# A planned order of instructions: other rates for transfers within device memory, and a slack for GpSimd

## The chip, the cores and the metric

The kernel runs on one core of one Trainium2 chip. The metric is the time of one execution in microseconds (us), as the device measures it. Three runs of the kernel before gave a median of 778.36 us (777.24 to 778.53).

The engines have short names in the profile: PE is TensorE's matmuls, PEld its weight loads, DVE is VectorE, ACT is ScalarE, POOL is GpSimd and SP is SyncE. POOLq and SPq are the queues on which POOL and SP issue transfers.

## The reference

All arrays are fp32; S = 2048, D = 512, F = 1792.

```python
x = A_x                                             # [1, 2048, 512]
g = sigmoid((x * gate_w).sum(-1, keepdims=True))
a = einsum("bsd,ed->bse", x, dft_hid_re)            # Fourier transform along D
b = einsum("bsd,ed->bse", x, dft_hid_im)
y = einsum("ts,bse->bte", dft_seq_re, a) - einsum("ts,bse->bte", dft_seq_im, b)   # along S, the real part
gate, up = x @ W_gate, x @ W_up
h = where(gate > 0, gate, 0) * up
return g * y + (1 - g) * (h @ W_down)
```

## The kernel before, in words

**Products.** Every fp32 operand is split into a high and a low part in a rounded form (ACT copies the high part, DVE subtracts for the low part), and a product is three passes of TensorE: high-high, high-low, low-high. A product of two by two blocks is made from seven block products (numbered 1 to 7) in place of eight, so sums and differences of blocks are formed on the way, of the weights, of x, and of the large matrices `cr` and `ci` (the transform along S). A matmul is 128 x 128 by 128 x 512.

**Stages, in TensorE's order.** First the blocks (`Block`) of gate and up: seven groups of weights times two halves q of x, with PSUM tiles named c. Each block makes two tiles h (`h0`, `h1`) and sums of them (`hs`), and `h_out` stores these to `hd` in device memory, from POOL (hd<-h, hd<-hs). Then the transform along D (tiles a, weights v, stored to `ad`), the last block, the product with W_down (`Down`, tiles z, operands hr loaded from `hd`), and then the transform along S: `Joint` 1, two `Sequence`s, `Joint` 3, two `Sequence`s, `Joint` 2 (tiles jA to jG, z).

**The sums of the large matrices.** The transform along S needs sums of blocks of `cr` and `ci`. For some of them the sums are formed long before, during the first stages, and kept in device memory as `tb`. There are two ways. `right_sums` (list `SUMS`) loads four blocks to tiles p, has DVE add them, and POOL stores them (tb<-p). `copied_sums` (list `DSUMS`, five entries) does it without the chip's own memory: POOL issues a transfer that copies a block of ci or cr to tb, and behind it a transfer that adds another block to it (`accum_op`). Four results 0, 2, 1, 3 make one entry, each a copy and an add. Result 1 begins as a copy of result 0 and result 3 as a copy of result 1 (tb<-tb), so result 0's copy and add, result 1's and result 3's follow each other, each waiting for the landing of the one before. The tb are first needed in the transform along S, at 485 us and later.

**Units.** On-chip memory is cut into 51 units of 4 KB per partition. Every tile takes a unit, and the unit of a finished tile is given to a new one. So a new tile's first write waits for the last use of the old one, which may be a store.

**Order.** The program is not run in the order in which it is written. Each step has a key: a place in time, in units of one 128 x 512 matmul of TensorE, to which it belongs. `Step` prices each step, `Queues` simulates the DMA queues (one of SP, one of POOL, which take turns packet by packet on 16 engines; a transfer lands `LANDING` us, and sometimes `BUSY` us more, after its last packet), `Plan.due` works out when each step has to be done, and `Plan.order` simulates the whole kernel and picks, for each engine, the step that can start first: when the steps it comes after are done, when its key has come (for DVE, ACT and SP 40 keys earlier, for POOL not before), and when a unit is free. Of steps that can start at nearly the same time the one that is due first goes first. What comes out is a fixed order of instructions on each engine and a fixed choice of units. On the chip each engine runs its list in order, and waits at an instruction until its inputs are there and its tile is free; what the planner supposed of times has no effect any more. In particular, a transfer on POOL that waits for another one's landing holds up the stores behind it.

`AT`, `SUMS` and `DSUMS` hold the keys that were set by hand: offsets for the opening, the weights of the opening (`w0`), the second half of x (`x`), the gate (`gate`), the transform's weights (`v`), the operands of the transform along S (`l0`, `l1`, `J1` to `J3`), the operands of a woven-in small product (`xt`), and the start of each entry of sums.

Of the kernel before, what the change touches and what calls it, by code (L numbers as in the profile page):

```python
# [11 lines left out]
OP = mybir.AluOpType  # L12
PSUM = bass.MemoryType.PSUM
DRAM = bass.MemoryType.DRAM
P = 128
# [47 lines left out]
class Buf:  # L63
# [17 lines left out]
    @property  # L81
    def all(self):
        return self[:]


class Step:


    def __init__(self, key, engine, name, a, k):
        self.key, self.engine, self.name, self.a, self.k = key, engine, name, a, k  # L90
        refs = [x for x in a if isinstance(x, Ref)]
        refs += [k[x] for x in ("out", "in_") if isinstance(k.get(x), Ref)]
        writes = [k["out"] if "out" in k else a[0]]
        if "accum_out" in k:
            writes.append(k["accum_out"])
        self.writes = [x for x in writes if isinstance(x, Ref)]
        self.reads = [x for x in refs if x is not writes[0]]
        if "accum_op" in k or name == "matmul" and not k["start"]:
            self.reads += self.writes
        self.after, self.start, self.end, self.due, self.rest = set(), None, None, None, None  # L100
        n = writes[0].size() if self.writes else 0
        self.hold = None
        if name == "tensor_copy":
            self.work = 0.1 + n * 0.52e-3
            self.hold = self.work - 0.05
        elif name == "dma_start":
            n = max(x.size() // (P if x.base.kind == "dram" else 1) for x in (*self.writes, *self.reads))
            self.work = n * 4 * P / 4096 * 0.160 / 16 * (2 if "accum_op" in k else 1)
        elif engine == "tensor":
            self.work = self.hold = 0.22667 * n / N  # L110
        elif engine == "vector":

            self.work = 0.156 + n * 1.039e-3
            self.hold = self.work - 0.083
        else:
            self.work = 0.19 + n * 0.845e-3
            self.hold = self.work - 0.09
# [8 lines left out]
class Queues:  # L126
# [32 lines left out]
    def add(self, step, start):  # L159

        def end(s, t, busy):
            s.end = t + self.LANDING + (self.BUSY if busy and t > self.EARLY else 0)

        self.now = self.serve(self.queues, self.now, max(start, self.now), end)
        packets = max(1.0, step.work / (0.160 / 16 * (2 if "accum_op" in step.k else 1)))
        self.queues.setdefault(step.engine, []).append([start, packets, step.work / packets, step])
        self.serve({e: [list(x) for x in q] for e, q in self.queues.items()}, self.now, 1e9, end)


class Plan:  # L170
# [9 lines left out]

    SUMS, STORES = 24, 0

    FREE = 30

    AHEAD = {"vector": 40, "scalar": 40, "sync": 40, "gpsimd": 0}

# [4 lines left out]
    def op(self, key, f, *a):  # L191
        self.ops.append((key, len(self.ops), f, a, self.rest))
# [58 lines left out]
    def order(self):  # L251
        todo = {}
        for s in self.steps:
            todo.setdefault(s.engine, []).append(s)
        for e in ("vector", "scalar"):
            todo[e].sort(key=lambda s: s.due)
        free, queues = dict.fromkeys(todo, 0.0), Queues()
        late, live, ends, over = 0.0, 0, [], []
        left = {b: len({id(x) for x in b.uses}) for b in self.bufs if b.kind == "unit"}
        done, begun, now = [], set(), 0.0  # L260

        turn = {s: n for n, s in enumerate(self.steps)}
        ahead = sorted(min(turn[s] for s in b.uses) for b in left if b.uses)
        while any(todo.values()):
            best = None
            for e, queue in todo.items():
                found = None
                near = queue[:1] if e == "tensor" or not queue else [*queue[:48], min(queue, key=turn.get)]
                for s in near:
                    if any(x.start is None for x in s.after):  # L270
                        continue
                    t = max(free[e], now)
                    for x in s.after:
                        t = max(t, x.end + (0 if x.engine == e else self.WAIT + 0.16 * (x.engine == "tensor")))
                    if e != "tensor":
                        t = max(t, (s.key - self.AHEAD[e] - self.FREE * (s.key > self.now - 200)) * self.MATMUL + late)
                    new = {r.base for r in (*s.writes, *s.reads) if r.base.kind == "unit" and r.base not in begun}
                    if new:
                        short = live + bisect_left(ahead, turn[s]) + len(new) - UNITS
                        if short > 0:  # L280
                            if len(ends) < short:
                                continue
                            t = max(t, ends[short - 1])
                    if found is None or t < found[0] - 0.12:
                        found = t, s, new
                if found and (best is None or found[0] < best[0]):
                    best = found
            if best is None:
                raise ValueError(f"no way on at {len(done)}: {[(e, q[0].key, q[0].name) for e, q in todo.items() if q]}")
            t, s, new = best  # L290
            now = t
            while over and ends[0] <= t:
                over.remove(min(over, key=Plan.last))
                ends.pop(0)
                live -= 1
            live += len(new)
            for b in new:
                ahead.remove(min(turn[x] for x in b.uses))
            begun |= new
            todo[s.engine].remove(s)  # L300
            s.start = t
            if s.name == "dma_start":
                free[s.engine] = t + self.ISSUE[s.engine]
                queues.add(s, free[s.engine] + self.LATE.get(s.engine, 0))
            else:
                s.end, free[s.engine] = t + s.work, t + s.hold
            if s.engine == "tensor" and s.key >= 0:
                late = max(late, t - s.key * self.MATMUL - 6 * self.MATMUL)
            for b in {r.base for r in (*s.writes, *s.reads) if r.base.kind == "unit"}:
                left[b] -= 1  # L310
                if not left[b]:
                    over.append(b)
            ends = sorted(map(Plan.last, over))
            done.append(s)
        self.steps = sorted(done, key=lambda s: s.start)
# [26 lines left out]
def kernel(ctx: ExitStack, tc, xP, xG, wgu, wd, cr, ci, wri, gw, out):  # L342
# [23 lines left out]
    dram = ctx.enter_context(tc.tile_pool(name="dram", bufs=1, space=DRAM))  # L366
# [4 lines left out]
    op, pe = plan.op, plan.pe  # L371
# [38 lines left out]
    def E():  # L410
        return plan
# [98 lines left out]
                op(key + k + 8 - (0 if n else early), w.lo, n, f)  # L510


    AT = {'open': (-19, 11, 33, 19, 97), 'w0': (17, 83, 126), 'x': (-184, -126, -85, -78, -51, -34, 35, 26), 'gate': (58, 44, 474), 'v': (-90, -80, -68, -38, -22, 4, 6, 34, 40), 'lw': (-246, -150, -138, -114, -112, -104), 'll': (-90, 62, 36, 96, 138, 176), 'l0': (-154, -58, -68, 16), 'l1': (-60, -118, -24, 40), 'z': (38,), 'J1': (88, 14, 76, 56, 116), 'J2': (174, 18, 40, 44, 52), 'J3': (168, 22, 52, 62, 52), 'hr': (52, 48, 61), 'rest': (26, 46), 'gated': (1880, 1930, 1968, 2008), 'xt': (-20, 10, 30), 'p': (62, 44, 32, 16), 'hs': (8, 6)}

    SUMS = {(0, 3, 1): 1764, (0, 1, 0): 865, (0, 2, 1): 675, (0, 3, 0): 985, (1, 1, 0): 1600, (1, 2, 1): 1602, (1, 5, 3): 1310, (1, 4, 2): 1070, (0, 4, 0): 489, (0, 1, 1): 125, (1, 4, 3): 1740}

    DSUMS = {(0, 2, 0): 290, (1, 2, 0): 100, (1, 3, 1): 427, (1, 3, 0): 645, (1, 1, 1): 520}

# [500 lines left out]
    def copied_sums(m, of, jj, key):  # L1021
        t = [tb[m, of - 1, jj, n] for n in range(4)]
        i = {b: (Joint if of < 4 else Sequence).source(m, of if of < 4 else of - 4, jj, b) for b in BLOCKS}
        for n, (o, a, b) in enumerate(((0, i["12"], i["22"]), (2, i["11"], i["12"]), (1, t[0], i["11"]), (3, t[1], i["21"]))):
            k = key + (0, 10, 50, 100)[n]
            op(k, lambda o=o, a=a: E().gpsimd.dma_start(out=t[o], in_=a, max_dma_last_dim=1024))
            op(k + 25, lambda o=o, b=b: E().gpsimd.dma_start(out=t[o], in_=b, accum_op=OP.add, max_dma_last_dim=1024))

    def gated(m, jj, g, key):
        r = buf("p")  # L1030
# [324 lines left out]
    w0, w1, w2 = Weights(0), Weights(1), Weights(2)  # L1355
# [184 lines left out]
```

## Time and profile before

| | |
|---|---|
| median of three runs | 778.36 us (777.24 to 778.53) |
| the profiled execution's own time | 779.43 us |
| its span, first to last instruction | 777.3 us |
| TensorE busy (PE) | 768.5 us (99%) |
| VectorE busy (DVE) | 697.7 us (90%) |
| ScalarE busy (ACT) | 499.7 us (64%) |
| GpSimd busy (POOL) | 140.4 us (18%) |
| DMA | 263.08 MB, 338 GB/s on the mean |
| transfers of POOL's queue (q0) | 100.15 MB, 42.3% of 16 engines' span |
| transfers of SP's queue (q1) | 162.17 MB, 54.2% |
| granted TensorE clock | 0.999 |

A row of a timeline has the start in us, the time in us, the engine, a line of the code (all steps run through one helper, so it is always the same), the operation, "out<-in" by the program's names without numbers, how many, and in brackets the idle time of the engine before it and what ended it. A row of waits has the engine and tile that waited, what for, and then us in total, how often, and the longest. A row of the DMA issues has out<-in, the queue, how many, KB each, and the median time from issue to landing. POOL and SP rows named DMA_DIRECT2D are the issuing of a transfer, not the transfer itself.

### The profile page before, as it was taken

The page shows a single profiled execution, that of the slowest core. Times are in us where ns is not written, and L with a number is a line of the kernel's source. Part 1 is how long each engine was busy: PE and PEld are TensorE (multiplying, and loading weights), DVE is VectorE, ACT ScalarE, POOL GpSimd, SP SyncE. Part 2 cuts the span into 40 slices and gives each one's busy share as a digit, 9 for nine tenths or more (in the row PEclk, how much of TensorE's full clock was granted, in tenths as well). Part 3 has the DMA queues.
Part 4 walks back from the last instruction along what each step waited for, and adds up shares of the span by engine and source line. Part 5 has one row for each costly group of instructions (what it writes and reads, how often), then busy time and mean ns, then how long its engine had stood idle before and what let it go on. Part 6 is the DMA issues. An engine that isn't in the chain of part 4 may idle for free.

```text
span 777.3 us, 10104 instructions
## 1 busy us (share of the span) xinstructions
PE 768.5 (99%) x3392; PEld 633.5 (81%) x3392; DVE 697.7 (90%) x812; ACT 499.7 (64%) x713; POOL 140.4 (18%) x204
## 2 busy tenths in 40 slices
PE   8999999999999999999999999999999999999998
PEld 6888888878788888888888888888888888888887
DVE  6999968676778986999979899999999999999997
ACT  6765574747475644666565568957567896566863
POOL 0123434342322222320202010001010001111000
PEclk9999999999999999999999999999999999999999
DMA  8966999999999899999999999999949899999993
GB/s 326 283 208 184 289 345 312 321 343 325 311 331 419 280 358 418 418 406 394 382 416 399 409 406 414 389 413 412 298 136 339 340 409 358 303 332 294 363 367 87
DMA packets 83683, 263.08 MB, mean 338 GB/s; under 512 B 8624, under 2 KB 19632, under 8 KB 83632
## 3 DMA queue, kind: packets, MB, share of 16 engines
q1 hardware_dynamic: 48048, 162.17, 54.2%
q0 software_dynamic: 35440, 100.15, 42.3%
q8 instruction: 26, 0.43, 0.2%
q14 instruction: 25, 0.20, 0.1%
q10 hardware_dynamic: 144, 0.13, 0.0%
HBM read 189.01 MB, written 94.38 MB: 365 GB/s over the span
## 4 chain that ended last, share of the span: by engine, by line
PE 74%; DMA 15%; DVE 7%; issue 2%; POOL 1%; SPq 1%; ACT 0%; POOLq 0%; DVEq 0%; ACTq 0%
PE z L123 40%; PE a L123 10%; PE c L123 10%; DMA tb<-ci 6%; PE jB L123 4%; PE jA L123 4%; DMA tb<-tb 4%; DMA tb<-cr 3%; PE jX L123 2%; PE jD L123 2%; DMA hd<-h 2%; DVE h L123 1%; PE jG L123 1%; DVE xl L123 1%; DMA wr<-wgu 1%
## 5 line engine op out<-in xcount | busy, mean ns | idle before, releaser
L123 PE MATMUL z<-cl,lh 128*128 128x512 f32 x452 | 175.9, 389 | 0.0
L123 PE MATMUL z<-ch,lh 128*128 128x512 f32 x452 | 175.8, 389 | 0.0
L123 PE MATMUL z<-ch,ll 128*128 128x512 f32 x452 | 175.8, 389 | 0.0
L123 DVE TENSOR_TENSOR jcl<-jr,jch 128x1024 fp32r<-128x1024 f32 x84 | 98.9, 1220 | 1.2 <-ACT jch L123 0.7
L123 PEld LDWEIGHTS z<-cl,lh 128*128 128x128 f32 x452 | 84.8, 188 | 17.8 <-DVE cl L123 0.2
L123 PEld LDWEIGHTS z<-ch,lh 128*128 128x128 f32 x452 | 84.8, 188 | 17.6
L123 PEld LDWEIGHTS z<-ch,ll 128*128 128x128 f32 x452 | 84.8, 188 | 17.6
L123 ACT CAST ch<-r 128x1024 fp32r<-128x1024 f32 x64 | 66.0, 1051 | 45.3 <-DVE r L123 30.5
L123 ACT CAST jch<-jr 128x1024 fp32r<-128x1024 f32 x84 | 84.3, 1052 | 8.1 <-PE z L123 3.2
L123 DVE TENSOR_TENSOR cl<-r,ch 128x1024 fp32r<-128x1024 f32 x64 | 77.2, 1220 | 0.4
L123 ACT CAST ch<-hr 128x1024 fp32r<-128x1024 f32 (+1 forms) x56 | 51.5, 944 | 31.8 <-PE z L123 17.5
L123 ACT ACTIVATE c<-c 128x512 f32<-128x512 f32 x74 | 42.8, 584 | 38.9 <-PE c L123 24.3
L123 DVE TENSOR_TENSOR cl<-hr,ch 128x1024 fp32r<-128x1024 f32 (+1 forms) x56 | 59.4, 1086 | 6.7 <-DMA hr<-hd 3.2
L123 DVE TENSOR_TENSOR p<-p,p 128x1024 f32<-128x1024 f32 x44 | 53.1, 1219 | 10.5 <-DMA p<-ci 5.5
L123 POOL DMA_DIRECT2D tb<-p x48 | 26.4, 559 | 110.1 <-DVE p L123 82.7
L123 PE MATMUL c<-xh,w1l 128*128 128x512 f32 x112 | 43.7, 390 | 1.9 <-ACT c L123 1.9
L123 PE MATMUL c<-xh,w2l 128*128 128x512 f32 x112 | 43.8, 391 | 1.6 <-DVE h L123 1.6
L123 PE MATMUL c<-xl,w1h 128*128 128x512 f32 x112 | 43.6, 389 | 0.0
L123 PE MATMUL c<-xl,w2h 128*128 128x512 f32 x112 | 43.6, 389 | 0.0
L123 PE MATMUL c<-xh,w2h 128*128 128x512 f32 x112 | 43.6, 389 | 0.0
L123 PE MATMUL a<-vh,xl 128*128 128x512 f32 x112 | 43.6, 389 | 0.0
L123 PE MATMUL a<-vl,xh 128*128 128x512 f32 x112 | 43.6, 389 | 0.0
(196 smaller groups left out, 1681.2 us busy)
## 6 DMA issues: line engine op xcount, KB each, us to landing
tb<-p POOLq DMA_DIRECT2D x48, 512.0 KB, 9.6
jr<-tb SPq DMA_DIRECT2D x48, 512.0 KB, 8.9
hr<-hd SPq DMA_DIRECT2D x36, 512.0 KB, 7.8
ad<-a POOLq DMA_DIRECT2D x28, 512.0 KB, 8.1
p<-cr SPq DMA_DIRECT2D x24, 512.0 KB, 9.6
tb<-ci POOLq DMA_DIRECT2D x24, 512.0 KB, 11.5
hd<-hs POOLq DMA_DIRECT2D x21, 512.0 KB, 10.1
r<-cr SPq DMA_DIRECT2D x21, 512.0 KB, 12.5
```

The costliest lines, as they stand in the source:

```text
L123: getattr(getattr(nc, self.engine), self.name)(*map(ap, self.a), **{k: ap(x) for k, x in self.k.items()})
```

## The change

The planner's arithmetic and its hand-set keys change; no step is added or removed. A transfer whose operands are all in device memory is priced 1.2 times as slow as one that is not (2.2 times where it adds, instead of 2). For a step on POOL that comes after a DMA, the planner counts the DMA as landed 3 us later than it otherwise would (`SLACK`; for DMAs that land after 20 us); POOL's list is ordered by that. In `copied_sums` the four copies start at keys 0, 20, 60 and 120 instead of 0, 10, 50 and 100, and an add is set 35 keys behind its copy instead of 25. Some entries of `AT`, `SUMS` and `DSUMS` move. In the list `AT`, cut here to the entries that differ:

```diff
         elif name == "dma_start":
             n = max(x.size() // (P if x.base.kind == "dram" else 1) for x in (*self.writes, *self.reads))
-            self.work = n * 4 * P / 4096 * 0.160 / 16 * (2 if "accum_op" in k else 1)
+            within = all(x.base.kind == "dram" for x in (*self.writes, *self.reads))
+            self.rate = 0.160 / 16 * ((2.2 if within else 2) if "accum_op" in k else 1.2 if within else 1)
+            self.work = n * 4 * P / 4096 * self.rate
...
-        packets = max(1.0, step.work / (0.160 / 16 * (2 if "accum_op" in step.k else 1)))
+        packets = max(1.0, step.work / step.rate)
...
+    SLACK = {"vector": 0, "scalar": 0, "gpsimd": 3}
...
                     for x in s.after:
                         t = max(t, x.end + (0 if x.engine == e else self.WAIT + 0.16 * (x.engine == "tensor")))
+                        if x.name == "dma_start" and x.end > 20:
+                            t = max(t, x.end + self.SLACK.get(e, 0))
...
-    AT = {... 'w0': (17, 83, 126), 'x': (-184, -126, -85, -78, -51, -34, 35, 26), 'gate': (58, 44, 474), 'v': (-90, -80, -68, -38, -22, 4, 6, 34, 40), 'l0': (-154, -58, -68, 16), 'l1': (-60, -118, -24, 40), 'J1': (88, 14, 76, 56, 116), 'J3': (168, 22, 52, 62, 52), 'gated': (1880, 1930, 1968, 2008), 'xt': (-20, 10, 30) ...}
-    SUMS = {... (0, 2, 1): 675, (0, 3, 0): 985, (1, 2, 1): 1602, (1, 4, 3): 1740}
-    DSUMS = {(0, 2, 0): 290, (1, 2, 0): 100, (1, 3, 1): 427, (1, 3, 0): 645, (1, 1, 1): 520}
+    AT = {... 'w0': (17, 83, 110), 'x': (-192, -134, -93, -86, -59, -42, 27, 18), 'gate': (66, 44, 474), 'v': (-90, -80, -68, -38, -22, 4, 10, 42, 44), 'l0': (-154, -42, -52, 32), 'l1': (-60, -118, -28, 40), 'J1': (88, 14, 76, 56, 124), 'J3': (168, 22, 62, 62, 52), 'gated': (1880, 1930, 1968, 2012), 'xt': (-20, 26, 62) ...}
+    SUMS = {... (0, 2, 1): 665, (0, 3, 0): 965, (1, 2, 1): 1632, (1, 4, 3): 1730}
+    DSUMS = {(0, 2, 0): 290, (1, 2, 0): 100, (1, 3, 1): 417, (1, 3, 0): 675, (1, 1, 1): 520}
...
         for n, (o, a, b) in enumerate(((0, i["12"], i["22"]), (2, i["11"], i["12"]), (1, t[0], i["11"]), (3, t[1], i["21"]))):
-            k = key + (0, 10, 50, 100)[n]
+            k = key + (0, 20, 60, 120)[n]
             op(k, lambda o=o, a=a: E().gpsimd.dma_start(out=t[o], in_=a, max_dma_last_dim=1024))
-            op(k + 25, lambda o=o, b=b: E().gpsimd.dma_start(out=t[o], in_=b, accum_op=OP.add, max_dma_last_dim=1024))
+            op(k+35, lambda o=o, b=b: E().gpsimd.dma_start(out=t[o], in_=b, accum_op=OP.add, max_dma_last_dim=1024))
```

More of the change, by code (lines that the diff above doesn't have):

```diff
@@ L510, in w_prep @@
                 op(key + k + 8 - (0 if n else early), w.lo, n, f)
-    AT = {'open': (-19, 11, 33, 19, 97), 'w0': (17, 83, 126), 'x': (-184, -126, -85, -78, -51, -34, 35, 26), 'gate': (58, 44, 474), 'v': (-90, -80, -68, -38, -22, 4, 6, 34, 40), 'lw': (-246, -150, -138, -114, -112, -104), 'll': (-90, 62, 36, 96, 138, 176), 'l0': (-154, -58, -68, 16), 'l1': (-60, -118, -24, 40), 'z': (38,), 'J1': (88, 14, 76, 56, 116), 'J2': (174, 18, 40, 44, 52), 'J3': (168, 22, 52, 62, 52), 'hr': (52, 48, 61), 'rest': (26, 46), 'gated': (1880, 1930, 1968, 2008), 'xt': (-20, 10, 30), 'p': (62, 44, 32, 16), 'hs': (8, 6)}
-    SUMS = {(0, 3, 1): 1764, (0, 1, 0): 865, (0, 2, 1): 675, (0, 3, 0): 985, (1, 1, 0): 1600, (1, 2, 1): 1602, (1, 5, 3): 1310, (1, 4, 2): 1070, (0, 4, 0): 489, (0, 1, 1): 125, (1, 4, 3): 1740}
-    DSUMS = {(0, 2, 0): 290, (1, 2, 0): 100, (1, 3, 1): 427, (1, 3, 0): 645, (1, 1, 1): 520}
+    AT = {'open': (-19, 11, 33, 19, 97), 'w0': (17, 83, 110), 'x': (-192, -134, -93, -86, -59, -42, 27, 18), 'gate': (66, 44, 474), 'v': (-90, -80, -68, -38, -22, 4, 10, 42, 44), 'lw': (-246, -150, -138, -114, -112, -104), 'll': (-90, 62, 36, 96, 138, 176), 'l0': (-154, -42, -52, 32), 'l1': (-60, -118, -28, 40), 'z': (38,), 'J1': (88, 14, 76, 56, 124), 'J2': (174, 18, 40, 44, 52), 'J3': (168, 22, 62, 62, 52), 'hr': (52, 48, 61), 'rest': (26, 46), 'gated': (1880, 1930, 1968, 2012), 'xt': (-20, 26, 62), 'p': (62, 44, 32, 16), 'hs': (8, 6)}
+    SUMS = {(0, 3, 1): 1764, (0, 1, 0): 865, (0, 2, 1): 665, (0, 3, 0): 965, (1, 1, 0): 1600, (1, 2, 1): 1632, (1, 5, 3): 1310, (1, 4, 2): 1070, (0, 4, 0): 489, (0, 1, 1): 125, (1, 4, 3): 1730}
+    DSUMS = {(0, 2, 0): 290, (1, 2, 0): 100, (1, 3, 1): 417, (1, 3, 0): 675, (1, 1, 1): 520}
     FORM = {1: 0, 2: 1, 3: 2, 5: 3, 7: 4, 6: 5, 4: 6}
```

## The prediction

> **What bounds the kernel now.** I read the page's head and part 1 first, then who TensorE waited for, then TensorE's own timeline around each wait, and from there backwards to the engine, the queue and the transfer behind it.
>
> ```profile
> span 777.3 us, 10104 instructions
> PE 768.5 (99%) x3392; PEld 633.5 (81%) x3392; DVE 697.7 (90%) x812; ACT 499.7 (64%) x713; POOL 140.4 (18%) x204
> PE c L123 <- ACT c L123: 1.9, 1, 1.9
> PE c L123 <- DVE h L123: 1.6, 1, 1.6
> PE warm L123 <- DVE warm L123: 1.1, 1, 1.1
> PE c L123 <- ACT w0h L123: 0.9, 2, 0.6
> 352.00 133.28 PE z L123 x588
> ```
>
> TensorE (PE) is busy for 99% of the span. All that it waited for stands in four rows. The last two are the warm-up and the first weights, at the very start, where nothing of the change reaches. The other two are single waits, and they alone are open to a new order. The last row is from the chain that ended last: 588 matmuls in 133.28 us are 0.2267 us each, which is the spacing of matmuls without a stall. With it the two waits can be priced by start times:
>
> ```profile
> 160.63 0.39 PE L123 MATMUL c<-xh,w1h 128*128 128x512 f32 x1
> 162.95 0.40 PE L123 MATMUL c<-xl,w2h 128*128 128x512 f32 x1
> 199.13 0.39 PE L123 MATMUL c<-xh,w1h 128*128 128x512 f32 x1
> 201.77 0.40 PE L123 MATMUL c<-xl,w1h 128*128 128x512 f32 x1
> ```
>
> (One matmul lies between the two of each pair.) The first stall costs 162.95 - 160.63 - 2 x 0.2267 = 1.87 us, the second 201.77 - 199.13 - 0.453 = 2.19 us; together 4.06 us. Behind each of them stands VectorE (DVE), and behind DVE a store:
>
> ```profile
> 143.97 0.68 DVE L123 TENSOR_TENSOR h<-g,c 128x512 f32<-128x512 f32 x1
> 161.87 0.69 DVE L123 TENSOR_TENSOR h<-c,y 128x512 f32<-128x512 f32 x1 [4.20 <-DMA hd<-h]
> 174.20 0.69 DVE L123 TENSOR_TENSOR h<-g,c 128x512 f32<-128x512 f32 x1 [0.17 <-ACT g L123]
> 200.07 0.69 DVE L123 TENSOR_TENSOR h<-c,y 128x512 f32<-128x512 f32 x1 [5.26 <-DMA hd<-h]
> 145.12 1.01 POOL L123 DMA_DIRECT2D tb<-ci  x1 [3.36 <-DMA tb<-ci]
> 145.74 1.71 POOL L123 DMA_DIRECT2D hd<-h  x2
> 182.15 0.66 POOL L123 DMA_DIRECT2D tb<-tb  x1 [4.10 <-DMA tb<-ci]
> 185.80 0.64 POOL L123 DMA_DIRECT2D tb<-tb  x1 [3.00 <-DMA tb<-ci]
> 186.44 1.29 POOL L123 DMA_DIRECT2D hd<-h  x2
> hd<-h POOLq DMA_DIRECT2D x1, 512.0 KB, 15.4
> 186.44 13.51 DMA hd<-h
> ```
>
> (The last two rows are from the DMA issues of 145.5 to 147.2 us and from the chain that ended last.) DVE wanted to write a new h at 161.87 - 4.20 = 157.7 us and at 200.07 - 5.26 = 194.8 us. The buffer was still being stored by an hd<-h that took 15.4 and 13.5 us to land. Both stores were issued late: GpSimd (POOL) issues in order, and it stood before a tb<-ci or tb<-tb transfer within device memory that waited for the landing of the one before it.
>
> **The change part by part.** The rates and the slack stand in the planner's arithmetic and add no instruction and no wait on the chip: the same 10104 instructions, the same matmuls, another order. So the gain can come only from the two stalls, and the loss only from new ones.
>
> *The rates.* A copy of 512 KB is 128 packets of 4 KB. The planner priced it at 128 x 0.160 / 16 = 1.28 us and now at 1.54; an add within device memory goes from 2.56 to 2.82. Each such step is taken 0.26 us longer. There are 40 of them (24 tb<-ci, 6 tb<-cr, 10 tb<-tb), so the plan counts on 10 us more of DMA work before about 220 us.
>
> *The slack.* Whatever POOL issues behind a DMA is taken as ready 3 us after the landing the planner expects, and another step that is ready sooner goes first. Whether 3 us is the right size can be read from what POOL waited for:
>
> ```profile
> POOL tb L123 <- DMA tb<-ci: 36.4, 11, 7.4
> POOL tb L123 <- DMA tb<-tb: 32.1, 10, 7.0
> POOL tb L123 <- DMA tb<-cr: 15.7, 3, 8.3
> tb<-ci POOLq DMA_DIRECT2D x24, 512.0 KB, 11.5
> tb<-tb POOLq DMA_DIRECT2D x10, 512.0 KB, 9.4
> ```
>
> (The last two rows are DMA issues of the page's part 6, with the median time to landing.) POOL's waits are 84.2 us in 24, 3.5 us each; slack and rate together are 3.26 us. So the mean wait is nearly covered, while the longest (7 to 8 us) are only halved.
>
> *The keys of the sums.* One key is one matmul, 0.2267 us. Copy to add goes from 25 to 35 keys (5.7 to 7.9 us), and the last add from 125 to 155 (28.3 to 35.1 us). Six transfers follow each other through five landings. Those took 11.5 us (tb<-ci) and 9.4 us (tb<-tb) by the median, so a chain lasts some 50 us in either kernel and landings, not keys, set it. I cost the keys at nothing in themselves; their effect is that a chain starts later or ends later, past the stores.
>
> *The first stall.* The last write of the stored h ends at 143.97 + 0.68 = 144.65, and the store goes at 145.74: up to 1.09 us of hold. The add issued at 145.12 stands ahead of it in the queue as well. What that is worth I take from the DMA view of the stretch:
>
> ```profile
> DMA packets 908, 1.97 MB, mean 303 GB/s; under 512 B 61, under 2 KB 554, under 8 KB 906
> DMA packets 1140, 1.70 MB, mean 261 GB/s; under 512 B 50, under 2 KB 951, under 8 KB 1140
> ```
>
> (139.5 to 146 us, and 180 to 186.5 us.) 512 KB at 303 GB/s are 1.73 us. If the add goes behind the store, this lands 1.09 + 1.73 = 2.8 us sooner, and 1.87 is what the stall needs. Without the second term 1.09 would leave 0.8 us of it. I take the whole 1.87 as gone; the margin is 0.9 us.
>
> *The second stall.* The 256 KB store, whose landing ended the wait, reads what DVE wrote at 174.20, long before. POOL was free at 182.15 + 0.66 = 182.81, stood 3.00 us for the second tb<-tb, and only then issued the store, at 186.44. Ahead of that copy the store goes 3.6 us sooner and has 512 KB less before it, which at 261 GB/s are 2.0 us. Of these 5.6 us the stall needs 2.19. It goes, and with more room than the first.
>
> The Trainium skill, "DMA: Bandwidth & Descriptors", section "Anatomy of one DMA — SWDGE (gpsimd) path", fits a transfer from GpSimd as about 2.0 us and its bytes over 436 GB/s, which is an estimate of 3.2 us for 512 KB. By that the stores would have landed long before DVE asked, and there would be no stall to remove; the trace does not agree, with 15.4 us.
>
> *The other keys.* Weights of the opening ("w0", 16 keys = 3.6 us earlier), the second x (8 keys earlier), the gate, "v", "l0", "l1", "J1", "J3" and four of the ordinary sums move by 8 to 32 keys (1.8 to 7.3 us). What hides them:
>
> ```profile
> 20.00:60.00 40.00, 40.00 (x177) 33.01 (x176) 39.97 (x51) 29.78 (x47) 9.61 (x13) 1.00 0.79 244
> 205.00:260.00 55.00, 55.00 (x244) 45.57 (x243) 46.62 (x62) 34.28 (x59) 14.60 (x23) 1.00 0.99 355
> 260.00:333.00 73.00, 73.00 (x323) 60.44 (x323) 61.07 (x88) 38.73 (x67) 21.78 (x32) 1.00 0.97 378
> 333.00:485.00 152.00, 152.00 (x672) 125.85 (x671) 143.26 (x152) 98.82 (x132) 18.17 (x32) 1.00 1.02 403
> 485.00:610.00 125.00, 125.00 (x553) 103.38 (x552) 124.67 (x125) 88.58 (x110) 8.61 (x12) 1.00 0.91 326
> GB/s 326 283 208 184 289 345 312 321 343 325 311 331 419 280 358 418 418 406 394 382 416 399 409 406 414 389 413 412 298 136 339 340 409 358 303 332 294 363 367 87
> ```
>
> (Stretch, then busy time of PE, PEld, DVE, ACT, POOL, then clock, DMA share, GB/s; the last row is the page's part 2, in 40 slices of the span.) PE is busy throughout in all five, so there is nothing to win there. Bounds: a gain of nothing, and a loss of one DVE step (0.6 to 1.3 us) for each that slips in front of one that PE needs, above all from 20 to 60 us, where DVE has 0.03 us free in 40. I take nothing, since the planner places DVE's steps by when they are due and these keys are only the earliest times.
>
> *The sum.* Two blocks now end in a small wait in place of a large one. Such small ones exist:
>
> ```profile
> PEld c L123 <- ACT c L123: 3.3, 4, 2.3
> DVE h L123 <- DMA hd<-h: 10.3, 3, 5.3
> ```
>
> (The second row is used at the end.) Three of the first row's four waits share 1.0 us, 0.3 each; I leave one 0.3 us in. So 4.06 - 0.3 = 3.8 us are won. The profiled execution took 779.43 us, 2.1 us more than its span, and would take 775.6; it lies 1.07 us above the median 778.36 of the runs, so the median becomes **774.6 us**.
>
> **The rivals.**
>
> *Only one stall goes.* For it: the margin of the first is 0.9 us out of terms of 1.09 and 1.73, and the second of these holds only if the add really lands behind the stores in the new order. If it stays ahead, most of the 1.87 us stays: 778.36 - 2.19 = 776.2 us. The Trainium skill, "DMA: Bandwidth & Descriptors", section "Issuing engines are not separate DMA queues", says that all issuers share the same 16 DMA engines, and that who issues saves only the sequencer's time; by that rule an earlier issue is worth its hold alone, which is this case. The trace agrees in so far as the DMA share from 205 to 485 us is about 1. Chance 0.15.
>
> *Nothing is won.* TensorE, 4 us ahead at 201 us, may run into transfers: the share is 0.97 to 1.02 from 260 to 485 us. Then the 4 us come back as waits for loads, at 778.4 us. Against it: slices of the page's part 2 reach 419 GB/s, at which the 403 x 152 of 333 to 485 us would take 146 us, 6 us less; and the rate falls to 326 behind it. The same time comes out if POOL's order around the two stores is as before, or if each stall only moves to another block. Chance 0.14.
>
> *Slower: the stalls multiply in the later blocks.* What goes behind the stores at 145 and 186 us goes in front of those after them:
>
> ```profile
> 196.58 1.12 POOL L123 DMA_DIRECT2D tb<-ci  x1 [7.04 <-DMA tb<-tb]
> 199.08 1.02 POOL L123 DMA_DIRECT2D tb<-ci  x1 [1.39 <-DMA tb<-tb]
> 199.75 0.94 POOL L123 DMA_DIRECT2D hd<-h  x1
> ```
>
> Here two adds already precede a store. The last chain now starts 30 keys (6.8 us) later and takes up to 3 us more at each of five landings, so it reaches from 220 to some 235 us, over two more blocks. Each late store is worth about 2.1 us, and it decides from where a store lands more than 2.3 us after DVE asks for the buffer (a wait of 4.20 us cost PE 1.87). Three such stalls in place of two: 778.36 + 2.1 = 780.5 us. The crowded DVE of 20 to 60 us would add to it. Against it: from 205 to 260 us the rate is 355 GB/s rather than 261 to 303, and PE lost nothing there. Chance 0.21.
>
> **How the numbers follow.** About 0.2% (1.6 us) is what a measurement of this kernel can tell from no change, so faster begins below 776.8 us. Forecast 0.50, all of it faster, by itself from 773.9 (nothing left of the stalls, and a little of the 0.2 us waits) to 775.8. One stall left, 0.15: two thirds faster, one third the same. Nothing won, 0.14: the same, but for 0.01. More stalls, 0.21: slower. So faster 0.60, the same 0.18, slower 0.22. The range goes from 773.8 to 780.4 us; above it is half of the slower case, below it some 0.05.
>
> **What would show it.** Right: no wait of PE over 0.5 us between 100 and 260 us; POOL's waits for tb<-ci, tb<-tb and tb<-cr well under 84 us in sum; the hd<-h stores at the two places issued ahead of a transfer within device memory, and DVE's waits for hd<-h (10.3 us in three in the page's list) nearly gone; PE spaced by 0.2267 us from 260 us on as before. Wrong: "DVE h <-DMA hd<-h" again ahead of a PE gap, at other blocks; a gap between 20 and 60 us behind a DVE step; a gap after 220 us whose releaser is a load; or landing times of hd<-h still at 13 us and more although POOL issued them on time, which would say that the queue and not the hold set them.

## The result, and the profile after

The changed kernel takes 775.44 us (median of 13 runs, 774.77 to 776.37) against 778.56 us (13 runs, 776.40 to 781.36) of the kernel before. The ratio is 0.996, with a 95% interval of 0.9947 to 0.9972: faster, by 3.1 us. Forecast were 774.6 us and a range of 773.8 to 780.4.

The first fence has rows of the page of the changed kernel: span and part 1. The second has all rows of what TensorE waited for, and POOL's waits for transfers of tb; columns as before (us in total, how often, the longest).

```profile
span 774.1 us, 10131 instructions
PE 768.3 (99%) x3392; PEld 634.1 (82%) x3392; DVE 698.6 (90%) x812; ACT 500.0 (65%) x713; POOL 141.3 (18%) x204
```

```profile
PE warm L125 <- DVE warm L125: 1.1, 1, 1.1
PE c L125 <- ACT w0h L125: 0.8, 1, 0.8
PE c L125 <- ACT c L125: 0.4, 1, 0.4
PE c L125 <- ACT g L125: 0.2, 1, 0.2
...
POOL tb L125 <- DMA tb<-ci: 23.0, 4, 9.4
POOL tb L125 <- DMA tb<-tb: 9.6, 3, 6.0
```

The profiled execution took 775.92 us, 774.1 of them span. Its span is 3.2 us shorter, and TensorE's work is the same. The page counts 10131 instructions, not the 10104 that the prediction took as the same; the counts in the second row are all as before, and the 27 more are semaphore instructions. The two rows of 1.9 and 1.6 us are gone, and of DVE's 10.3 us of waiting for hd<-h nothing is left in the list. Two short waits stand in their place. POOL's waits behind tb fell from 84.2 us in 24 to 32.6 us in 7.

TensorE's timeline shows both short waits:

```profile
51.67 0.39 PE L125 MATMUL c<-xh,w2h 128*128 128x512 f32 x1
52.27 0.50 PE L125 MATMUL c<-xh,w2l 128*128 128x512 f32 x1 [0.21 <-ACT g L125]
52.61 0.40 PE L125 MATMUL c<-xl,w2h 128*128 128x512 f32 x1
...
181.88 0.39 PE L125 MATMUL c<-xh,wnt 128*128 128x512 f32 x1
182.62 0.50 PE L125 MATMUL c<-xt1h,w0l 128*128 128x512 f32 x1 [0.35 <-ACT c L125]
182.95 0.39 PE L125 MATMUL c<-xt1l,w0h 128*128 128x512 f32 x1
```

By start times, the way the prediction did it, they cost 52.61 - 51.67 - 0.453 = 0.49 us and 182.95 - 181.88 - 0.453 = 0.62 us. I did the same with every matmul's start. Beyond 0.2267 us each, TensorE lost between 140 and 205 us 4.66 us before and 0.65 us after, and between 20 and 60 us 0.07 us before and 0.81 us after. So 4.0 us were won where the stalls had been and 0.7 us were lost in the opening. The first 20 us lost 0.3 us more than before, and the stretch from 60 to 140 us 0.2 us less, which makes up the 3.2 us of the spans.

### The profile page after: what moved, and what is told of

Same layout as the page of the kernel before. It is cut to its first block, busy times and chain, and to the rows that moved or that the text cites. A ratio compares the mean times of both kernels' runs of the same rounds, so it can differ in the third digit from the quotient of the medians.

```text
span 774.1 us, 10131 instructions
## 1 busy us (share of the span) xinstructions
PE 768.3 (99%) x3392; PEld 634.1 (82%) x3392; DVE 698.6 (90%) x812; ACT 500.0 (65%) x713; POOL 141.3 (18%) x204
## 4 chain that ended last, share of the span: by engine, by line
PE 90%; DVE 5%; DMA 2%; ACT 1%; issue 1%; SPq 1%; ACTq 0%; DVEq 0%
PE z L125 40%; PE c L125 26%; PE a L125 10%; PE jB L125 4%; PE jA L125 4%; DMA wr<-wgu 2%; PE jX L125 2%; PE jD L125 2%; PE jG L125 1%; DVE wr L125 1%; PE jH L125 1%; DVE h L125 1%; DVE p L125 1%; DVE xl L125 1%; SPq L125 1%
## 5 line engine op out<-in xcount | busy, mean ns | idle before, releaser
L125 PE MATMUL c<-xh,w1h 128*128 128x512 f32 x112 | 43.6, 389 | 0.0
```

Source lines behind the costliest of these rows:

```text
L125: getattr(getattr(nc, self.engine), self.name)(*map(ap, self.a), **{k: ap(x) for k, x in self.k.items()})
```

## The experiments

The two stalls are called after the time at which they begin in the kernel before: **160** and **199**. Two theories were to be told apart. **T** (time) is the prediction's: the stores of h are issued and land earlier, so the buffer is free when DVE asks. **U** (unit) came up when I worked out from the code which unit the planner gives each tile. In the kernel before, the h of 160 lies in the unit of an earlier h whose 512 KB store it waits for, and the h of 199 in the unit of the h with the 256 KB store. In the changed kernel they lie in the units of a p and of a weight tile (wr), and no store stands before them. By U the stalls went because the planner, expecting later landings, freed other units first.

Three comparisons shared the kernel before on one chip each. It took 779.71 us there (experiments 1 to 4, 35 runs), 780.69 us (5 to 8, 25 runs) and 779.87 us (9 to 12, 19 runs). The ratios are to these.

### 1 to 4: one or two parts of the change alone

**1, rates and slack** (the kernel before with these hunks):

```diff
+            self.rate = 0.160 / 16 * ((2.2 if within else 2) if "accum_op" in k else 1.2 if within else 1)
+    SLACK = {"vector": 0, "scalar": 0, "gpsimd": 3}
+                            t = max(t, x.end + self.SLACK.get(e, 0))
```

> The kernel before with the new rates and GpSimd's slack, its old keys and tables. In its order the two stores of h at about 145 us go ahead of the adds, as the prediction wanted, but the h that stalled at 160 us still lies in the unit that such a store frees; the h that stalled at 199 us lies in another unit, one that no store frees. Theory T (time: stores issued and landed earlier end both stalls): no PE wait over 0.5 us from 140 to 205 us. Theory U (unit: the stalls went because the planner, expecting later landings, gave h another unit): a wait of about 1.9 us at 160 us stays, the one at 199 us is gone; median about 776.5 us.

Measured: 775.89 us, ratio 0.9958 (0.9942 to 0.9974). The h of 160 lies in the same kind of unit as before, and no stall is left there. DVE's and POOL's timelines, and then the DMA issue of that store:

```profile
159.09 0.68 DVE L125 TENSOR_TENSOR h<-c,y 128x512 f32<-128x512 f32 x1
145.60 0.76 POOL L125 DMA_DIRECT2D hd<-h  x1 [9.61 <-DVE h L125]
146.35 2.19 POOL L125 DMA_DIRECT2D tb<-ci  x2
```

```profile
hd<-h POOLq DMA_DIRECT2D x1, 512.0 KB, 7.2
```

POOL now waits for h itself (9.61 us) and issues the store as soon as it is written, ahead of two adds. It lands in 7.2 us where it took 15.4, and DVE's write has no wait. T holds at 160, U does not. One wait of 0.7 us, for w2l at 183 us, is new.

**2, slack alone** (the second and third line above, without the rates).

> The kernel before with the slack alone. One add goes between the two stores of h at 145 us and holds the second of them, so by T the stall at 160 us stays or grows (1.9 us and more). Both h lie in units that no store frees, so by U both stalls are gone: about 774.5 to 775.5 us.

Measured: 777.02 us, 0.9969 (0.9959 to 0.9979). No wait for h was left. TensorE lost 0.33 us from 140 to 165 us and 0.35 from 165 to 205; one wait of 0.4 us stands at 213 us. An add went ahead of the later store of h, so T alone would have kept 160. U has it. The time is 1.5 to 2.5 us above what U gave; where its runs lost that is open, since its profile (776.48 us) shows only the short waits.

**3, tables alone** (the new `AT`, `SUMS` and `DSUMS`, nothing else).

> The kernel before with the new hand-set tables alone. The first store of h at 182 us goes ahead of one of the two copies, so by T the stall at 199 us is gone or at most 0.5 us. The h there still lies in the unit that this store frees, while the one of 160 us doesn't, so by U the stall at 199 us stays at 1 to 2 us and that at 160 us is gone: about 776.3 us.

Measured: 778.58 us, 0.9989 (0.9966 to 1.0013): no change that can be told. At 160 nothing was lost (another unit). At 199 DVE waited 3.6 us for hd<-h in the unit of the store, but with the store ahead of one copy TensorE lost only 0.44 us: T had that right and U did not. The time went elsewhere, in waits at 57, 214 and 270 us (0.45, 0.85 and 0.77 us).

**4, keys inside an entry alone**:

```diff
-            k = key + (0, 10, 50, 100)[n]
+            k = key + (0, 20, 60, 120)[n]
-            op(k + 25, lambda o=o, b=b: E().gpsimd.dma_start(out=t[o], in_=b, accum_op=OP.add, max_dma_last_dim=1024))
+            op(k+35, lambda o=o, b=b: E().gpsimd.dma_start(out=t[o], in_=b, accum_op=OP.add, max_dma_last_dim=1024))
```

> The kernel before with the new keys inside an entry of sums alone (0, 20, 60, 120 and 35). GpSimd's order around both stores is as before, two copies ahead of the stores at 182 to 186 us, so by T both stalls stay: 778.4 us. The h of 199 us lies in a unit freed by an older store of hs, 4 us earlier by the plan, that of 160 us as before, so by U the stall at 160 us stays (1.9 us) and that at 199 us is gone: about 776.3 us.

Measured: 778.43 us, 0.998 (0.9966 to 0.9995). At 160 (same unit, same order) 1.08 us were lost from 140 to 165 us, at 199 (another unit, same order) nothing. U had both places right. New waits at 211 and 215 us (0.5 and 1.4 us) took the gain, so its time was 2 us off.

Each theory missed twice where it was taken as the only way out: T at 160 in 2 and at 199 in 4, U at 160 in 1 and at 199 in 3. Read together, the four agree on more: at these two places a stall of about 1 us or more stood only where the tile lay in a late store's unit *and* the store went behind waiting adds or copies.

### 5 and 6: each theory by itself

Here the planner's result of the kernel before was kept, and one thing was changed by hand after it. In **5** every tile keeps its unit, and two transfers of POOL change places. The edits of 5 and 6 are given in words here, not in code.

```diff
+        # units as chosen for the old order; then, in the list of steps:
+        move(add with key 555, to behind the store of h with key 617)
+        move(256 KB store of h with key 781, to ahead of the copy with key 695)
```

> The kernel before, every tile in the unit it had, and two transfers of GpSimd alone put elsewhere in its order: the add that went at 145.12 us goes behind the two stores of h, and the 256 KB store of 186.44 us goes ahead of the second tb<-tb copy. Theory T (time): the stall at 160 us needs its store 1.87 us sooner and gets about 2.8, the one at 199 us needs 2.19 and gets about 5.6; both gone, about 774.5 to 775.5 us against 779 of the kernel before on the same chip. Theory U (unit): both stay, no difference.

Measured: 779.33 us, 0.998 (0.9961 to 0.9998). Both stalls are gone, and two thirds of the gain are not there. The timeline of DVE and POOL at both places and of TensorE behind them, and then the issues of the two stores with their landing times:

```profile
159.09 0.69 DVE L123 TENSOR_TENSOR h<-c,y 128x512 f32<-128x512 f32 x1 [1.14 <-DMA hd<-h]
197.43 0.69 DVE L123 TENSOR_TENSOR h<-c,y 128x512 f32<-128x512 f32 x1 [3.06 <-DMA hd<-h]
145.22 0.76 POOL L123 DMA_DIRECT2D hd<-h  x1 [2.39 <-DVE h L123]
182.51 0.55 POOL L123 DMA_DIRECT2D hd<-h  x1
182.68 0.50 PE L123 MATMUL c<-xt1h,w0l 128*128 128x512 f32 x1 [0.98 <-ACT c L123]
212.97 0.39 PE L123 MATMUL c<-xh,w 128*128 128x512 f32 x1
214.85 0.50 PE L123 MATMUL c<-xt1h,wnt 128*128 128x512 f32 x1 [1.49 <-ACT c L123]
215.19 0.40 PE L123 MATMUL c<-xt1l,wnt 128*128 128x512 f32 x1
```

```profile
hd<-h POOLq DMA_DIRECT2D x1, 512.0 KB, 13.8
hd<-h POOLq DMA_DIRECT2D x1, 256.0 KB, 14.8
```

DVE waited 1.14 us where it had waited 4.20, and 3.06 where it had been 5.26; TensorE has work for that long, and nothing was lost from 140 to 165 us nor at 199. So T's mechanism is real, and enough at both places. But the next thing was late: 1.3 us at 183 us and 215.19 - 212.97 - 0.453 = 1.77 us at 215 us. The timeline has what stands ahead of these two: a row of DVE at 179 us that waited 0.51 us for weights, and at 209 us a row of ACT and three sums of DVE:

```profile
179.39 0.69 DVE L123 TENSOR_TENSOR wr<-wr 128x512 f32<-128x512 f32 x1 [0.51 <-DMA wr<-wgu]
...
209.51 1.07 ACT L123 COPY s<-c 128x512 f32<-128x512 f32 x2 [1.38 <-DMA hd<-h]
209.91 3.61 DVE L123 TENSOR_TENSOR p<-p,p 128x1024 f32<-128x1024 f32 x3
213.45 0.68 DVE L123 TENSOR_TENSOR h<-g,c 128x512 f32<-128x512 f32 x1
```

The copy to s waited for another store of h, and DVE put three sums ahead of the h that ACT's next instruction on c waited for. Two hand-made moves mend two places; behind them the order waits for other landings, of weights and of another store.

In **6** the order stays, and two tiles exchange units:

```diff
+        # after the units are chosen: from here on the two units change names
+        swap(unit of h1 with key 819, unit of p11 with key 821)
```

> The kernel before, every instruction in the order it had, and two tiles exchanged in place: the h of 199 us lies in the unit of the block p loaded just before it (freed by a store of hs, issued 9 us sooner than that of h), and that p in the unit which the store of 186.44 us frees. U: the stall at 199 us is gone (or the new cause stands in its place), that at 160 us stays: about 2.2 us less than the kernel before. T as the only way out: both stay, since the store lands as late as it did.

Measured: 779.02 us, 0.9974 (0.9956 to 0.9993). The timeline of DVE at both places, of POOL at the second and of TensorE at 138 us, and then the issue of the store:

```profile
163.61 0.69 DVE L123 TENSOR_TENSOR h<-c,y 128x512 f32<-128x512 f32 x1 [3.72 <-DMA hd<-h]
198.11 0.69 DVE L123 TENSOR_TENSOR h<-c,y 128x512 f32<-128x512 f32 x1 [0.67 <-PE c L123]
189.06 1.29 POOL L123 DMA_DIRECT2D hd<-h  x2
136.52 0.39 PE L123 MATMUL c<-xh,w 128*128 128x512 f32 x1
138.47 0.50 PE L123 MATMUL c<-xt1h,wnt 128*128 128x512 f32 x1 [1.57 <-ACT c L123]
```

```profile
hd<-h POOLq DMA_DIRECT2D x1, 256.0 KB, 12.4
```

160 stays, with a wait of 3.72 us of DVE. At 199 the store was issued as late as ever and landed at 189.06 + 12.4 = 201.5 us, 3.4 us after DVE's write, which did not care: U is enough there by itself. Of the 2.2 us expected 1.7 came. TensorE's two rows are a surprise: up to 189 us this kernel has the list of instructions and the units of the kernel before, which lost 0.2 us between 100 and 140 us in its profile, and here 138.47 - 136.52 - 0.227 = 1.72 us went in one gap. (The profiled execution of 6 is one of its longer ones, 780.85 us.) So the stalls of the old order seem to differ from one execution to another in place and size.

### 7 to 12: the change without one of its parts

**7, without the slack** (`SLACK` of 0 for GpSimd).

> The changed kernel without GpSimd's slack: new rates, keys and tables. T, with the slack as the part that does the work: GpSimd stands before adds again (over 50 us in sum, against 33 in the changed kernel and 84 before) and at least one wait of PE for h of 1 us or more comes back, 777 us or more. U: neither h lies in a unit that a late store of h frees, so 775.5 us as with the slack.

Measured: 777.55 us (8 runs), 0.9949 (0.993 to 0.9968). Neither stall is back, and POOL waited 49.1 us behind tb (28.0, 19.8 and 1.3), between 32.6 and 84.2. A wait of 1.7 us for w2l stands at 185 us, behind weights that DVE waited 1.84 us for. T's time came true, by another wait than T's. The changed kernel was not run on this chip; by its 775.44 and 775.63 us on two others the slack is worth some 2 us. The ratio hides this, since the kernel before was slower here.

**8 and 10, the old keys of the opening**, measured on two chips, the second beside the changed kernel (**9**):

```diff
-    AT = {... 'w0': (17, 83, 110), 'x': (-192, -134, -93, -86, -59, -42, 27, 18) ...}
+    AT = {... 'w0': (17, 83, 126), 'x': (-184, -126, -85, -78, -51, -34, 35, 26) ...}
```

> The changed kernel with the old keys of the opening (w0: 126 in place of 110, and the eight old keys of x). If the waits of PE at 52 and 56 us (0.7 us together) come from VectorE's steps w1l and xl that these keys put ahead of the h that PE needs, they go, and with nothing new it takes about 774.8 us, 0.7 less than the changed kernel. If they come from something else (transfers in the opening), they stay.

> The changed kernel once more, on one chip with the three below. If the kernel before differs from chip to chip and run to run (778.6 to 780.7 us so far) because its stalls do, and the changed kernel has little left to stall, this takes 775.4 us again whatever the kernel before takes here.

> The changed kernel with the old keys of the opening, once more: 774.9 us, 0.5 to 0.7 less than the changed kernel beside it, with no wait of PE over 0.3 us after 20 us.

Measured: 774.89 us (5 runs), 0.9911 (0.9888 to 0.9934), and 774.70 us (6 runs, 774.48 to 775.28), 0.9936 (0.9916 to 0.9956). The changed kernel beside the latter took 775.63 us (7 runs, 775.19 to 776.61), 0.9948 (0.993 to 0.9966). The fences have DVE's and then ACT's timeline of the changed kernel at 50 us, and the window from 20 to 60 us of the changed kernel and then of 8 (busy PE, PEld, DVE, ACT, POOL, clock, DMA share, GB/s):

```profile
49.89 1.22 DVE L125 TENSOR_TENSOR xl<-x,xh 128x1024 fp32r<-128x1024 f32 x1
51.02 1.22 DVE L125 TENSOR_TENSOR w1l<-wr,w1h 128x1024 fp32r<-128x1024 f32 x1
52.16 0.68 DVE L125 TENSOR_TENSOR h<-c,s 128x512 f32<-128x512 f32 x1
49.61 1.07 ACT L125 CAST w1h<-wr 128x1024 fp32r<-128x1024 f32 x1
51.60 0.62 ACT L125 ACTIVATE g<-c 128x512 f32<-128x512 f32 x1
```

```profile
20.00:60.00 40.00, 39.79 (x175) 32.22 (x174) 39.92 (x49) 29.42 (x47) 8.31 (x12) 1.00 0.74 214
```

```profile
20.00:60.00 40.00, 40.00 (x179) 33.04 (x178) 39.97 (x50) 29.83 (x47) 8.19 (x12) 1.00 0.75 217
```

With the new keys xl and w1l (1.22 us each) go ahead of an h on DVE, and on ACT the cast w1h goes ahead of g. It was this g, not the h of 52.16 us, that ended TensorE's wait at 52.27 us. With the old keys the h and the g come at 49.1 and 49.3 us, ahead of all three, and TensorE runs through. That the keys are the cause is shown by 8 and 10; which of the steps that they move does it is not. After 20 us neither 8 nor 10 shows a wait of TensorE in its list. This version is 0.9 us below the changed kernel beside it (0.5 to 0.7 were expected), with ranges that barely touch, and so faster than both kernels.

**11, the old rates, and 12, the old tables**, each with all the rest of the change:

> The changed kernel with the old rates (1 and 2). One add (key 730) goes right ahead of the stores of h at 182 us again, and the h of 199 us lies in the unit that such a store frees. T: a wait of 1 us or more comes back at about 199 us, 776.5 to 777 us. If the slack alone puts the stores in time, no wait there: 775.4 us, as the changed kernel.

> The changed kernel with the old hand-set tables (new rates, slack and keys inside the sums). The stores of h at 145 us go ahead of two adds, while the h of 160 us lies in the unit that such a store frees: by T no wait at 160 us, by U 1.9 us. If the tables do nothing but fit, 775.4 us; if they carry a share of the gain, 776 us and more.

Measured: 777.56 us, 0.9973 (0.9958 to 0.9988), and 775.35 us (7 runs), 0.9948 (0.9929 to 0.9968). Rows of who waited, of 11 and then of 12:

```profile
DVE h L123 <- DMA hd<-h: 3.1, 1, 3.1
PE c L123 <- ACT c L123: 1.0, 2, 0.6
```

```profile
PE c L125 <- ACT w0h L125: 0.5, 1, 0.5
PE c L125 <- DVE w2l L125: 0.2, 1, 0.2
```

Without the rates DVE waits for a store again (at 197 us), though TensorE loses nothing there; its waits stand at 175 and 214 us. The time is 0.6 us above what T said, and the place is another, so T failed here, and so did the slack alone (775.4 us). Without the new tables nothing is lost: the h of 160 lies in a store's unit there, and there is no stall. That is T at this place once more. On this chip the rates are worth 1.9 us (777.56 to 775.63), the tables -0.3 us, which is within the spread of the runs. That -0.3 is a sum of two: the tables' keys of the opening cost 0.9 us (10), so their other entries won about 0.65 (775.35 to 774.70).

## Why the prediction was right

**Two stalls, both gone.** Their price (1.87 and 2.19 us) was right: 4.0 us were won between 140 and 205 us. No wait in the list between 100 and 260 us is over 0.5 us, POOL's waits fell to 39% of what they were, and TensorE's spacing after 260 us is as before, as the last part of the prediction asked.

**The first stall's working: the sum was right, its split was not.** The store was to land 2.8 us sooner, 1.09 of them hold (POOL standing before another transfer) and 1.73 queue (a transfer ahead of the store). In experiment 5 it did: DVE's write, right behind the landing, began at 159.09 in place of 161.87 us. But the trace gives the queue all of it. In each of the fourteen traces all of POOL's 199 transfers landed in the order in which they were issued, so a store lands behind whatever stands ahead of it. The landing times of the kernel before show what that costs; the rows are two tb<-ci, issued at 140.62 and 145.12 us (the latter is the add that went ahead of the store), and the two tb<-tb of 182.15 and 185.80 us:

```profile
tb<-ci POOLq DMA_DIRECT2D x1, 512.0 KB, 16.2
tb<-ci POOLq DMA_DIRECT2D x1, 512.0 KB, 14.3
tb<-tb POOLq DMA_DIRECT2D x1, 512.0 KB, 13.9
tb<-tb POOLq DMA_DIRECT2D x1, 512.0 KB, 12.7
```

The first tb<-ci landed at 156.8 us and the add at 159.4, 2.6 us behind it. With the add behind the store, these 2.6 us are nearly the whole gain. Of the 1.1 us by which the store was issued sooner hardly anything can be seen in it. (The row at 145.74 us in the prediction holds two stores; DVE waited for the second, of 512 KB, issued at 146.32.)

**The second stall's working was mis-sized.** 5.6 us were worked out: 3.6 of hold and 2.0 of queue. In experiment 5 the store was issued 3.9 us sooner (182.51 for 186.44), but it took 14.8 us instead of 13.5, so it landed 2.6 us sooner, from 199.95 to 197.3. The row of the one tb<-tb that stood ahead of it there, issued at 181.87 us:

```profile
tb<-tb POOLq DMA_DIRECT2D x1, 512.0 KB, 14.0
```

It landed at 195.9 us, and the store 1.4 us later. In the kernel before the two tb<-tb landed at 196.0 and 198.5, and the store again 1.4 us later. So the term of 2.0 us for the queue measured 2.5, and the term of 3.6 us for the hold measured next to nothing. A store that is issued sooner does not pass what POOL has already put into the queue. The Trainium skill, "DMA: Bandwidth & Descriptors", section "Two DMAs through the same engine are not ordered", says that within one queue of one DMA engine descriptors start in order, and promises no order of their writes; in these traces the landings kept the order too. What was won sufficed because the stall needed only 2.19: a margin of 0.4 us, not 3.4. In the changed kernel the store stands ahead of both tb<-tb.

**What the prediction did not see is the unit.** It took for granted that the new h would ask for the same buffer. In the changed kernel it doesn't: the stores at 145.33 and 174.37 us still took 13.1 and 15.4 us to land, which the prediction's own last sentence names as a sign that the queue and not the hold sets the landing, and so it was. Yet nothing waited for them. DVE's writes of the two h in the changed kernel:

```profile
160.89 0.68 DVE L125 TENSOR_TENSOR h<-c,y 128x512 f32<-128x512 f32 x1
194.51 0.69 DVE L125 TENSOR_TENSOR h<-c,y 128x512 f32<-128x512 f32 x1 [0.67 <-PE c L125]
```

The stores had landed at 158.4 and 189.8 us, before these writes. So in this trace they were in time even for the old units. The rates and the slack changed what the planner expects, and that changed both the order and the units. Experiments 5 and 6 show that either suffices at 199. At 160 experiments 1, 5 and 12 show it for time alone, and experiment 2, in whose order an add goes ahead of the store, speaks for the unit; the unit alone wasn't tried there. In 2, in 3 and in the changed kernel DVE's order at 160 differs as well (another h goes first), so none of these three isolates the unit. The changed kernel has both the earlier landing and the other unit; by its trace either would have been enough.

**The other keys, taken as nothing, cost 0.7 us.** This is the term that, for the most part, made the forecast 0.8 us too low. (Some of these keys move by 4 only, not by 8 to 32.) A gap between 20 and 60 us was one of the prediction's signs of being wrong, and it came. Its bound was right (one DVE step of 0.6 to 1.3 us that slips in front, above all from 20 to 60 us), and the reason for choosing nothing was wrong: the planner orders DVE by when steps are due, but the new keys let the steps of weights and x start earlier, and in a stretch where DVE has 0.08 us free in 40 they went ahead of an h and, on ACT, of the g that TensorE waited for. Experiment 10 gives 0.9 us back. The 0.3 us left in for a small wait stood for 0.62 us in one profile and for none in another.

**The rivals.** "Only one stall goes" failed on both stalls. Its argument, that an earlier issue is worth its hold alone, came out the other way round: the place in the queue was worth 2.6 and 2.5 us, and the hold next to nothing. "Nothing is won" failed: TensorE waits for nothing after 205 us. "The stalls multiply in the later blocks" failed for the change. But waits further on did take two thirds of the gain of experiment 5, at 183 us behind weights and at 215 us behind a late store of h.

## What to carry to other kernels

Where a fixed order and a fixed choice of buffers come from a model of times, a wrong duration in the model hurts twice: in-order engines stand before transfers that have not landed, and buffers are given away as free that are not. Where the queue holds work all the time, as here around both stalls, what counts for a store is which transfers stand ahead of it, not when it is issued. Mending the model's durations, with a margin on the one engine that stands before landings, did more (775.35 to 775.89 us in experiments 1, 9 and 12) than moving the two guilty transfers by hand (779.33). Probably it mends the places that would have been late next as well: in 7, without the margin, and in 11, without the new durations, waits of 0.4 to 1.7 us stood at other places. After it, look again at the stretches where another engine is full: a key that only allows an earlier start is not free there.

## What the runs showed that I had not expected

- **The old order is not one time.** The kernel before took 776.4 to 785.6 us over its runs on these chips, the changed one 774.8 to 776.6. Profiles of nearly the same list lost 0.2 and 2.0 us between 100 and 140 us (the kernel before, and experiment 6). The changed order is narrower as well as faster. The slack alone does not explain that: experiments 1 and 11 have it, and their longest runs took 779.24 and 779.65 us.
- **The landing of the same kind of store depends on what stands ahead of it in POOL's queue.** 512 KB of h took 15.4 us behind an add (the kernel before), 13.8 with the last add taken away, and 7.2 where POOL had stood idle 9.6 us before it (experiment 1). At 264.59 us in the kernel before it took 3.3 us.
